# Masking the last 64 queries of each head with GpSimd and an accumulating DMA instead of VectorE

## The chip, the core and the metric

The kernel runs on one core of a Trainium2 chip. The core has a matrix engine (TensorE, PE, with its weight loads shown apart as PEld), a vector engine (VectorE, DVE), a scalar engine for activations (ScalarE, ACT), GpSimd (POOL) and SyncE (SP), which here only starts DMAs. Each engine works through its own queue in order; engines wait for each other by semaphores. Data lie in SBUF (128 partitions) and, for matrix results, in PSUM. The metric is the time of one execution on the device in microseconds (us), as the median of several runs.

## What is computed

Attention over 4 batches of 8 heads, 576 positions, head width 64, with scores far below a row's maximum masked away, then two feed-forward layers:

```python
scores = scale * np.matmul(q, k.transpose(0, 1, 3, 2))
thresh = np.max(scores, axis=-1, keepdims=True) - tau
scores = np.where(scores >= thresh, scores, -1000000000.0)
scores = scores - np.max(scores, axis=-1, keepdims=True)
attn = np.exp(scores)
attn = attn / (np.sum(attn, axis=-1, keepdims=True) + 1e-09)
return np.matmul(attn, v).astype(np.float32)
...
h = x @ w_in
g = np.maximum(h, 0.0) + alpha * np.minimum(h, 0.0)   # second layer: h * sigmoid(h)
return (g @ w_out).astype(np.float32)
```

The feed-forward layers take 2304 tokens of width 512 through 2048 inner columns. Everything is float32.

## The kernel before

The program has two parts that follow each other in each queue: attention, and the two feed-forward layers.

*Units of attention.* Heads are taken two at a time; there are 16 such pairs (`pairs`, index `i`). A unit is a tile of 128 queries or of 2 x 64 queries against all 576 keys. A pair has units `t` = 0 to 7 for its first 512 queries. The last 64 queries of two neighbouring pairs share two more units, `t` = 8 and 9, which are counted with the even `i`; so there are 144 units, and 16 of them have `t` above 7. One unit passes through these steps:

- `qkmm`: PE writes the scores of two units to PSUM (line 576).
- `maxi` (L589, DVE): reads the scores from PSUM, writes them negated and scaled to an SBUF tile `x`, and gathers each row's minimum, which is the maximum of the scores. Four tiles `x` are used in turn (`XB`).
- `thr` (L602, POOL): adds `tau`, for two units at once.
- `expo` (L599, ACT): exponential of `x` into a part of a tile `e`; a tile holds two units, six tiles are used in turn (`EB`).
- `mask` (L608, DVE): sets to zero what lies beyond the threshold, and sums the row.
- `recip` (L614, DVE) and `spread`, `spread8` (L618, L622, POOL copies to `rb`): one over the sum, spread to 64 columns.
- `trans` (L651, PE): transposes of `e` and `rb`, by banks `T0`, `T2`, `T4`, `T6`, `Te` for a pair and `T8`, `T9` for the shared units; `copy` (L307, ACT) brings them to SBUF as `pt`, `pe`, `p8`, `p9`.
- `pv` (L672) and `pv8` (L680), PE: the product with the values; `evac` (L692, L711, ACT) writes it to `X`, and `norm`, `norm8` (L703, L715, POOL) multiply by the reciprocal.

Between them lie parts of the feed-forward layers: the conversion of seven weight tiles (`conv`; on DVE L390, L392 and L394, on POOL L408 and L413), the preparation of the first inputs (`piece`, L445 and L455), and the first four feed-forward products (`h`, line 465). At the very start the PE works on zeros (`idle`, L518): `WU` such fillers ahead of the first scores, `WF` after them.

*What sets the order.* `op(name, engine, duration, priority, dependencies, function, finish)` only records a step. `TABLE1` is a list of numbers that gives the order in which the steps are issued; `plan` walks through it with the durations noted in `op` and so gives each engine its sequence. `ORDER` names the sequence of banks. Steps marked `DVE+` and `POOL+` are those that the planner keeps from running at the same time; in the program that becomes a wait of the POOL step for the `DVE+` step planned before it. A step marked `POOL` gets no such wait. `recip` and `max` are plain `DVE`. The feed-forward layers have `TABLE2` and `SIDE`, which the change leaves as they are.

*The feed-forward layers.* Each runs in groups of inner columns over three parts of 768 tokens, with a scheme of seven products in place of eight; every product is made of three matrix products of split float32 numbers. PE loads weights (L465) for each. Some sums there are made by an accumulating DMA from POOL's queue (L1021).

Of the kernel before, what the change touches and what calls it, by code (L numbers as in the profile page):

```python
# [90 lines left out]
def mode(n):  # L91
# [11 lines left out]
    "352u2x2+BL399+303336FIBMBOBN3A3CFPBPBRHgHf380MBQ0N3FHeBS9-3DHhBUFQBTBVHiHjBX3H3K3BA03NBZBYFR3EBWFS3L"
    "3I3P3G3SHk0IFU3MFJ3JHlFKBaHm3V3a3Q3OHnFV3XBb3T3bBd3R3d3UHo3W3YHpHqFW3fBeBc3iBg013Z3cBh3j3lBi3eFLFX3g"
    "3n3o3k3h3qFYFZBfFTBjHrFaHsHtA1A23tHuBkBmFc3mHv3r3v3yBl3sBn0L3pHwBoBp3z3-44413w3uHxBq3xHy0P42453+Hz0Q"
    "BrFg40Bs47FhH+Fi49Bt4CA34A4F4D0O46434KBuH-48BvBwI0FjBxBy4L4H4N4E4BBzB-B+FbC04SI1I3Fk0TC1I2I4A4I54GC2"
# [1138 lines left out]
```

## Time and profile before

| | us |
|---|---|
| median of 3 runs | 959.94 (959.6 to 960.05) |
| the profiled execution | 959.58 |
| its span in the trace | 957.8 |
| PE busy in the span (modelled ends) | 946.3 |
| PE weight loads busy | 849.6 |
| DVE busy | 843.9 |
| ACT busy | 617.8 |
| POOL busy | 335.1 |

The span runs from the first to the last instruction of one execution; some 1.8 us of the execution lie outside it. Busy shares are averages over both parts of the program: attention lies in the first quarter of the span, up to about 249 us, the feed-forward layers behind it. The granted clock of TensorE is 1.00 of full speed (2.4 GHz) throughout.

### The profile page before, as it was taken

How to read it: one execution, taken by the hardware profiler on the slowest of the kernel's cores; microseconds unless marked ns; L12 is line 12 of the kernel's file. 1: busy time of each engine (PE TensorE's matmuls, PEld its weight loads, DVE VectorE, ACT ScalarE, POOL GpSimd, SP SyncE). 2: the span in 40 equal slices, each digit the busy share in tenths (PEclk: the TensorE clock that was granted, in tenths of full speed). 3: DMA queues.
4: the chain of work that ended last, by engine and by line, in shares of the span. 5: the costliest groups of instructions: out<-in, count | busy, mean ns of one | idle time of the engine just before them, and what ended most of it. 6: DMA issues, size and time to landing. Idle time of an engine off the chain costs nothing.

```text
span 957.8 us, 18332 instructions
## 1 busy us (share of the span) xinstructions
PE 946.3 (99%) x6810; PEld 849.6 (89%) x6810; DVE 843.9 (88%) x1672; ACT 617.8 (65%) x1096; POOL 335.1 (35%) x401
## 2 busy tenths in 40 slices
PE   8999999999999999999999999999999999999998
PEld 4565566665899999999999999999999999999998
DVE  7999999999688668999999999999888888887866
ACT  5889999898767655555555555767664555455442
POOL 0235533445523214453333453301214332323344
PEclk9999999999999999999999999999999999999999
DMA  3132232222667676858667886558685667557543
GB/s 102 35 118 96 77 108 72 70 79 95 227 253 266 241 276 224 274 194 320 230 228 274 261 258 212 184 211 313 241 334 188 242 242 290 177 212 287 178 146 140
DMA packets 46073, 190.99 MB, mean 199 GB/s; under 512 B 5408, under 2 KB 8736, under 8 KB 45984
## 3 DMA queue, kind: packets, MB, share of 16 engines
q1 hardware_dynamic: 44016, 184.81, 54.0%
q0 software_dynamic: 1728, 4.72, 2.7%
q8 instruction: 54, 0.88, 0.4%
q10 hardware_dynamic: 240, 0.30, 0.1%
q14 instruction: 35, 0.29, 0.1%
HBM read 147.33 MB, written 37.75 MB: 193 GB/s over the span
## 4 chain that ended last, share of the span: by engine, by line
PE 93%; DVE 3%; ACT 2%; issue 1%; POOL 0%; DVEq 0%; ACTq 0%; POOLq 0%
PE ab L465 30%; PE c L465 18%; PE y L465 17%; PE s L576 8%; PE pv L672 8%; PE y L958 5%; PE t L651 5%; ACT e L599 1%; PE t L680 1%; PE pv L518 1%; ACT pt L307 1%; DVE x L589 1%; DVE X L975 0%; DVE r L445 0%; DVE e L608 0%
## 5 line engine op out<-in xcount | busy, mean ns | idle before, releaser
L465 PE MATMUL ab<-xs,w 128*128 128x384 f32 x1728 | 326.2, 335 | 0.0
L465 PEld LDWEIGHTS ab<-xs,w 128*128 128x128 f32 x1728 | 302.0, 188 | 2.0 <-DVE e L608 0.8
L465 PE MATMUL y<-g,w 128*128 128x384 f32 x840 | 163.7, 335 | 0.0
L465 PEld LDWEIGHTS y<-g,w 128*128 128x128 f32 x840 | 147.4, 188 | 0.0
L307 ACT ACTIVATE g<-r 128x768 fp32r<-128x768 f32 (+1 forms) x143 | 111.6, 794 | 46.7 <-DVE r L1024 11.5
L408 POOL TENSOR_TENSOR cw<-cw 128x128 f32<-128x128 f32 (+1 forms) x89 | 49.4, 555 | 228.5 <-DVE cw L408 87.8
L307 ACT ACTIVATE su<-ab 128x384 f32<-128x384 f32 x144 | 68.7, 488 | 85.5 <-PE ab L465 66.2
L465 PE MATMUL c<-g,w 128*128 128x384 f32 x612 | 119.8, 335 | 0.0
L608 DVE SCALAR_TENSOR_TENSOR e<-x,m,e 128x577 f32<-128x577 f32 x144 | 116.6, 845 | 0.3 <-POOL m L602 0.2
L589 DVE TENSOR_SCALAR_CACHE_REDUCE x<-s,nsc 128x576 f32<-128x576 f32 x144 | 112.0, 812 | 4.0 <-PE s L576 3.0
L599 ACT ACTIVATE e<-x,m 128x576 f32<-128x576 f32 x144 | 107.9, 779 | 11.5 <-DVE x L589 11.4
L465 PEld LDWEIGHTS c<-g,w 128*128 128x128 f32 x612 | 107.4, 188 | 0.0
L1010 POOL TENSOR_TENSOR g<-r,g 128x768 fp32r<-128x768 f32 x40 | 73.8, 1849 | 74.5 <-DVE cw L408 11.6
L576 PE MATMUL s<-raw 64*128 64x288 f32 (+1 forms) x640 | 98.5, 422 | 0.5 <-DVE x L589 0.4
L975 DVE TENSOR_TENSOR X<-y,X 128x384 f32<-128x384 f32 x150 | 81.2, 551 | 18.7 <-PE y L465 17.9
L651 PEld LDWEIGHTS t<-ident,e 64*128 64x128 f32 x1296 | 56.5, 138 | 46.0 <-ACT pt L307 25.1
L1010 DVE TENSOR_TENSOR g<-r,g 128x768 fp32r<-128x768 f32 x81 | 81.7, 1012 | 4.9 <-ACT g L307 4.8
L465 PE MATMUL c<-xs,w 128*128 128x384 f32 x432 | 84.1, 335 | 0.7 <-ACT r L929 0.7
L576 PEld LDWEIGHTS s<-raw 64*128 64x128 f32 (+1 forms) x640 | 58.6, 177 | 24.8 <-DVE x L589 15.7
L307 ACT ACTIVATE pt<-t 128x512 f32<-128x512 f32 x128 | 71.8, 598 | 9.5 <-PE t L651 9.2
L465 PEld LDWEIGHTS c<-xs,w 128*128 128x128 f32 x432 | 75.7, 188 | 1.1 <-ACT r L929 1.1
L307 ACT ACTIVATE w<-cw 128x896 fp32r<-128x896 f32 (+1 forms) x64 | 59.7, 932 | 24.4 <-POOL cw L408 12.4
(93 smaller groups left out, 1411.3 us busy)
## 6 DMA issues: line engine op xcount, KB each, us to landing
xs<-xd SPq DMA_DIRECT2D x126, 768.0 KB, 5.7
xd<-xs SPq DMA_DIRECT2D x42, 768.0 KB, 4.3
raw<-in_w1i SPq DMA_DIRECT2D x16, 512.0 KB, 5.4
raw<-in_w1o SPq DMA_DIRECT2D x16, 512.0 KB, 5.3
raw<-in_w2i SPq DMA_DIRECT2D x16, 512.0 KB, 5.5
raw<-in_w2o SPq DMA_DIRECT2D x16, 512.0 KB, 4.9
rv<-in_v SPq DMA_DIRECT2D x16, 320.0 KB, 3.3
r<-r POOLq DMA_DIRECT2D x12, 384.0 KB, 5.7
```

The lines of the kernel that those rows point to most:

```text
L307: e.activation(out=dst, in_=src, func=AF.Copy)
L408: st.append((both_step if both else port_step)(256 if len(o.shape) == 3 else 128, ["cv", "ce", "ch"], ["ce"], lambda e=V, o=o, a=a, b=b, o ...
L465: T.matmul(bank, WT_[ws[c]][:, x, AI[a], :], xs[:, y, c, :], start=start and k == 0, stop=stop and k == 5, skip_group_check=True,)
L576: T.matmul(SP[u + k][o, hf, :S // 2], RAW[i + n][p, 0, q], RAW[i + n][p, 1, c], start=True, stop=True)
L589: V.tensor_scalar(out=x.rearrange("p (a b) -> p a b", a=2), in0=SP[u][:, :, :S // 2], scalar1=nsc, scalar2=None, op0=ALU.mult, op1=ALU.min ...
L599: A.activation(out=ES[u], in_=xts[u % XB][:, 1:S + 1], func=AF.Exp, bias=mcol(u, 0), scale=-1.0)
L608: return V.scalar_tensor_tensor(out=e, in0=x, scalar=mcol(u, 1), in1=e, op0=ALU.is_le, op1=ALU.mult, accum_out=mcol(u, 2))
L651: T.transpose(TP[n][h][:, c * 64:c * 64 + 64], x[p], ident[p, p])
L672: T.matmul(AV[i][h * 64:(h + 1) * 64], RV[i][:, h, kt], probs(i, h, kt).rearrange("p a b -> p (a b)"), start=kt == 0, stop=kt == KT - 1)
L958: T.matmul(yt, wview(ws[f])[:, a, i * 128:(i + 1) * 128], half(gs[f, k])[:, c], start=n == 0, stop=n == 3 * G - 1)
L975: V.tensor_tensor(out=dst, in0=src, in1=dst, op=ALU.add))))
L1010: add(*both_step(2 * HN, kr + kg, kg, lambda e: e.tensor_tensor(out=x[:, 1], in0=RP[n], in1=x[:, 0].bitcast(F32), op=ALU.subtract)))
```

## The change

The two shared units of a pair (`t` above 7) no longer use the mask on DVE. In its place, ahead of the exponential: POOL compares the negated scores with the threshold and writes 1e30 where a score is beyond it, zero elsewhere, to a tile `bm` (`above`); a DMA issued by POOL adds `bm` onto the score tile (`raise_`); the exponential of what was raised is zero; and ACT writes the row's sum along with the exponential. POOL then adds 1e-9 to that sum (`eps`), and DVE takes these two reciprocals apart from the other eight (`recip8`). The units have score tiles of their own, two in turn (`PMB`, `xm0` and `xm1`), one single `bm`, and their own tile `e`; the other tiles `e` become five. `sm` has three buffers in place of four. There is one start filler fewer (`WU`). Some durations noted for the planner are other numbers, and `TABLE1` and `ORDER` are new, so the order of the attention part is another on every engine. The order of the feed-forward part is the same.

```diff
 XB = 4
-EB = 6
+EB = 5
+PMB = 2
-WU = 9
+WU = 8
...
-    "P8:1 P8:0 T4:1 Q2:2 P4:0 T6:1 Q4:2 T2:1 Te:1 Q6:2 P0:1 P1:1 Q8:2 T0:2 P2:1 T4:2 Q0:3 P3:1 T2:2 Q2:3 T6:2 P4:1 "
+    "Q2:2 T6:1 P4:0 Te:1 Q4:2 P0:1 P1:1 Q6:2 T8:0 P2:1 T2:2 Q8:2 P3:1 T0:2 Q0:3 T4:2 P4:1 T9:0 Q2:3 P8:0 P8:1 Te:2 "
...
-        sm = ent(name="sm", bufs=4)
+        sm = ent(name="sm", bufs=3)
-        eb = qp.tile([128, EB, 2 * S + 2], F32, tag="e", name="e")
+        eb = qp.tile([128, EB + 1, 2 * S + 2], F32, tag="e", name="e")
...
+        PMU = {u: n for n, u in enumerate(x for x in range(NU) if seq[x][1] > 7)}
+        xms = [rbp.tile([128, S], F32, tag=f"xm{k}", name=f"xm{k}") for k in range(PMB)]
+        bm = rbp.tile([128, S], F32, tag="bm", name="bm")
...
+        def above(u):
+            P.tensor_scalar(out=bm, in0=xt(u), scalar1=mcol(u, 1), scalar2=1e30, op0=ALU.is_gt, op1=ALU.mult)
+
+        def raise_(u):
+            P.dma_start(out=xt(u), in_=bm, accum_op=ALU.add)
+
+        def eps(u):
+            P.tensor_scalar(out=mcol(u, 2), in0=mcol(u, 2), scalar1=1e-9, scalar2=None, op0=ALU.add)
...
-            A.activation(out=ES[u], in_=xts[u % XB][:, 1:S + 1], func=AF.Exp, bias=mcol(u, 0), scale=-1.0)
+            A.activation(out=ES[u], in_=xt(u), func=AF.Exp, bias=mcol(u, 0), scale=-1.0, **({"accum_out": mcol(u, 2)} if u in PMU else {}))
...
         def recip(i):
-            n = 8 if i % 2 else 10
-            V.reciprocal(stat(i)[:, 2, :n], stat(i)[:, 2, :n])
+            V.reciprocal(stat(i)[:, 2, :8], stat(i)[:, 2, :8])
+
+        def recip8(i):
+            V.reciprocal(stat(i)[:, 2, 8:], stat(i)[:, 2, 8:])
...
+            if u in PMU:
+                last = PML[PMU[u] - 1] if PMU[u] else -1
+                op(("above", u), "POOL", 1.93, 2, [("thr", i, t - t % 2), ("raise", last)], lambda u=u: above(u), 2.08)
+                op(("raise", u), "SWD", 0.9, 2, [("above", u)], lambda u=u: raise_(u), 6.5)
+                op(("eps", u), "POOL", 0.2, 2, [("exp", u)], lambda u=u: eps(u), 0.35)
-            op(("exp", u), "ACT", 0.667, 2, [("max", u)] + (users(*etiles[n]) if n >= 0 else []), lambda u=u: expo(u), 0.82)
-            op(("mask", u), "DVE+", 0.74, 2, [("exp", u), ("thr", i, t - t % 2)], lambda u=u: mask(u), 0.9)
+            op(("exp", u), "ACT", 0.667 + 0.19 * (u in PMU), 2, [("max", u)] + [("raise", u)] * (u in PMU) + ring, lambda u=u: expo(u), 0.82 + 0.19 * (u in PMU))
+            if u not in PMU:
+                op(("mask", u), "DVE+", 0.74, 2, [("exp", u), ("thr", i, t - t % 2)], lambda u=u: mask(u), 0.9)
...
-            op(("spread", i), "POOL", 0.6, 1, [("recip", i)] + ([("t", bank[i - 1, "e"])] if i else []), lambda i=i: spread(i), 0.75)
+            op(("spread", i), "POOL", 0.88, 1, [("recip", i)] + ([("t", bank[i - 1, "e"])] if i else []), lambda i=i: spread(i), 1.03)
             if i % 2 == 0:
-                op(("spread8", i), "POOL", 0.25, 1, [("recip", i)] + ([("t", bank[i - 2, "9"])] if i else []), lambda i=i: spread8(i), 0.4)
+                op(("recip8", i), "DVE", 0.12, 0, [("eps", pos[i, x]) for x in (8, 9)], lambda i=i: recip8(i), 0.25)
+                op(("spread8", i), "POOL", 0.46, 1, [("recip8", i)] + ([("t", bank[i - 2, "9"])] if i else []), lambda i=i: spread8(i), 0.6)
```

In the rows below the first number of a name's ending is a buffer: `m_530` before and `m_507` after hold the statistics of pair `i` = 2. First DVE, from the maxima of that pair's shared units on; before:

```order
L589 TENSOR_SCALAR x3_172,m_530<-s_681,nsc_68 128x576
L589 TENSOR_SCALAR x2_169,m_530<-s_680,nsc_68 128x576
L608 SCALAR_TENSOR_TENSOR e_162,m_530<-x0_163,m_530,e_162 128x577
L608 SCALAR_TENSOR_TENSOR e_162,m_530<-x1_166,m_530,e_162 128x577
L589 TENSOR_SCALAR x0_163,m_757<-s_744,nsc_68 128x576
L589 TENSOR_SCALAR x1_166,m_757<-s_745,nsc_68 128x576
L608 SCALAR_TENSOR_TENSOR e_162,m_530<-x3_172,m_530,e_162 128x577
L608 SCALAR_TENSOR_TENSOR e_162,m_530<-x2_169,m_530,e_162 128x577
L589 TENSOR_SCALAR x3_172,m_757<-s_781,nsc_68 128x576
L589 TENSOR_SCALAR x2_169,m_757<-s_780,nsc_68 128x576
L614 RECIPROCAL m_530<-m_530 128x10
```

The same place on DVE after the change:

```order
L609 TENSOR_SCALAR xm1_187,m_507<-s_674,nsc_68 128x576
L609 TENSOR_SCALAR xm0_186,m_507<-s_673,nsc_68 128x576
L636 RECIPROCAL m_211<-m_211 128x2
L628 SCALAR_TENSOR_TENSOR e_162,m_507<-x3_172,m_507,e_162 128x577
L609 TENSOR_SCALAR x1_166,m_745<-s_715,nsc_68 128x576
L609 TENSOR_SCALAR x0_163,m_745<-s_714,nsc_68 128x576
L628 SCALAR_TENSOR_TENSOR e_162,m_507<-x2_169,m_507,e_162 128x577
L633 RECIPROCAL m_507<-m_507 128x8
L609 TENSOR_SCALAR x2_169,m_745<-s_759,nsc_68 128x576
L609 TENSOR_SCALAR x3_172,m_745<-s_760,nsc_68 128x576
```

The two masks of the shared units are gone; the reciprocal of the pair before's shared units stands between the maxima and a mask.

POOL at that place, before (thresholds L602, copies of reciprocals L618 and L622, products with the reciprocal L703 and L715):

```order
L602 TENSOR_SCALAR m_530<-m_530,ptau_67 128x2 x2
L602 TENSOR_SCALAR m_757<-m_757,ptau_67 128x2
L618 COPY rb_836<-m_530 128x512
L703 TENSOR_TENSOR X0_69<-X0_69,pe_663 128x256
L602 TENSOR_SCALAR m_757<-m_757,ptau_67 128x2 x2
L622 COPY rb8_892<-m_530 128x128
```

And after (comparison L538, its DMA L541; thresholds L622, copies L640 and L644, products L725 and L737):

```order
L622 TENSOR_SCALAR m_507<-m_507,ptau_67 128x2 x2
L644 COPY rb8_721<-m_211 128x128
L538 TENSOR_SCALAR bm_188<-xm0_186,m_507 128x576
L541 DMA xm0_186<-bm_188 128x576
L640 COPY rb_771<-m_507 128x512
L622 TENSOR_SCALAR m_745<-m_745,ptau_67 128x2 x2
L737 TENSOR_TENSOR X0_69<-X0_69,p9_766 128x2x64
L725 TENSOR_TENSOR X0_69<-X0_69,pe_602 128x256
L622 TENSOR_SCALAR m_745<-m_745,ptau_67 128x2
L538 TENSOR_SCALAR bm_188<-xm1_187,m_507 128x576
L541 DMA xm1_187<-bm_188 128x576
```

Two comparisons and two DMAs have come in, ahead of copies and thresholds of the pairs that follow.

ACT, from the exponential of unit `xm0` of that pair on, after the change (before, the two stand as `e_162<-x3_172,m_530` and `e_162<-x2_169,m_530`, four rows apart and ahead of all exponentials of the next pair):

```order
L619 ACTIVATE e_162,m_507<-xm0_186,m_507 128x576
L390 ACTIVATE cw_84<-raw0_83 128x512
L308 ACTIVATE pt_890<-t_946 128x8x64
L619 ACTIVATE e_162<-x0_163,m_936 128x576
L308 ACTIVATE pt_890<-t_947 128x8x64
L308 ACTIVATE pt_890<-t_975 128x8x64
L619 ACTIVATE e_162<-x1_166,m_936 128x576
L308 ACTIVATE pt_890<-t_976 128x8x64
L714 ACTIVATE X0_69<-pv_887 128x512
L619 ACTIVATE e_162,m_507<-xm1_187,m_507 128x576
```

The two exponentials now stand behind all eight of the next pair (`m_745`), and the second behind two of the pair after that (`m_936`).

PE at the end of attention, before, up to the feed-forward layers:

```order
L680 MATMUL t<-p_3501,rv 64x64 x8
L680 MATMUL t<-p_3587,rv 64x64 x2
L672 MATMUL pv<-pt,rv 64x512 x2
L465 MATMUL ab_3647<-xs_79,w_72 128x384 x3
L465 MATMUL ab_3647<-xs_79,w_73 128x384 x3
L651 MATMUL t<-ident,e 128x64 x16
L672 MATMUL pv<-pe,rv 64x512 x2
```

and after:

```order
L673 MATMUL t<-ident,rb 128x64 x8
L694 MATMUL pv<-pt,rv 64x512 x8
L673 MATMUL t<-ident,e 128x64 x16
L694 MATMUL pv<-pe,rv 64x512 x2
L673 MATMUL t<-ident,e 128x64 x2
L673 MATMUL t<-ident,rb_3774 128x64 x2
L466 MATMUL ab_3650<-xs_80,w_74 128x384 x3
L466 MATMUL ab_3650<-xs_80,w_75 128x384 x3
L702 MATMUL t<-p_3780,rv 64x64 x8
L702 MATMUL t<-p_3798,rv 64x64 x2
```

The products of the last shared units (L680, now L702) stood ahead of the last pair's last banks, and now stand with their transposes at the very end; of the four early feed-forward products one has moved forward.

## Rows read from the trace of the kernel before

**Rows 1.** Windows: us, busy us (instructions) of each engine, granted clock, DMA.

```profile
core 0: us, PE busy (x) PEld busy (x) DVE busy (x) ACT busy (x) POOL busy (x), PEclk, DMA share, GB/s
40.00:60.00 20.00, 19.37 (x200) 10.55 (x199) 19.90 (x54) 17.69 (x31) 5.75 (x13) 1.00 0.26 78
120.00:140.00 20.00, 19.96 (x254) 12.92 (x252) 20.00 (x53) 18.26 (x35) 7.67 (x18) 1.00 0.27 77
200.00:220.00 20.00, 19.93 (x260) 12.16 (x258) 19.94 (x54) 19.30 (x38) 10.73 (x24) 1.00 0.21 65
260.00:280.00 20.00, 20.00 (x117) 20.00 (x116) 18.11 (x31) 16.20 (x34) 3.97 (x4) 1.00 0.61 246
```

**Rows 2.** Waits of DVE, 20 to 235 us: for whom, us, times, longest.

```profile
DVE x L589 <- PE s L576: 0.7, 2, 0.6
DVE x L589 <- PE t L651: 0.2, 1, 0.2
DVE e L608 <- POOL m L602: 0.2, 1, 0.2
```

**Rows 3.** Chain of waits, 22 to 245 us, shares by line.

```profile
by line: PE pv L672 30.8%; PE s L576 30.5%; PE t L651 22.2%; PE t L680 3.5%; ACT e L599 3.2%; ACT pt L307 2.8%; issue 2.0%; PE ab L465 1.1%; DVE x L589 0.8%; POOL cw L408 0.5%; ACT pe L307 0.5%; ACT w L307 0.4%; DVE e L608 0.4%; DVE cw L394
```

**Rows 4.** Groups by line and shape, 10 to 240 us: count, busy, mean ns, idle before.

```profile
L608 DVE SCALAR_TENSOR_TENSOR e<-x,m,e 128x577 f32<-128x577 f32 x143 | 115.9, 845 | 0.3 <-POOL m L602 0.2
...
L703 POOL TENSOR_TENSOR X<-X,pe 128x256 f32<-128x256 f32 x12 | 8.7, 735 | 9.4 <-DVE e L608 9.4
...
L703 POOL TENSOR_TENSOR X<-X,pe 128x192 f32<-128x192 f32 x12 | 7.2, 596 | 7.6 <-DVE e L608 7.6
```

**Rows 5.** Lines L608 (masks) and L618 (copies): shortest, median, longest ns.

```profile
L608 DVE SCALAR_TENSOR_TENSOR e<-x,m,e x144: 757/816/1271, 10.5 to 240.0; 128x577 f32<-128x577 f32 x144
...
L618 POOL COPY rb<-m x16: 609/988/1196, 24.7 to 241.2; 128x512 f32<-128x512 f32 x16
```

**Rows 6.** Timeline of attention, DVE and POOL: start us, us, what.

```profile
142.96 0.61 POOL L618 COPY rb<-m 128x512 f32<-128x512 f32 x1
...
143.78 0.29 POOL L622 COPY rb<-m 128x128 f32<-128x128 f32 x1
...
163.15 0.81 DVE L608 SCALAR_TENSOR_TENSOR e<-x,m,e 128x577 f32<-128x577 f32 x1
...
163.89 0.81 DVE L608 SCALAR_TENSOR_TENSOR e<-x,m,e 128x577 f32<-128x577 f32 x1
...
172.75 0.21 DVE L614 RECIPROCAL m<-m 128x10 f32<-128x10 f32 x1
...
173.01 0.82 DVE L608 SCALAR_TENSOR_TENSOR e<-x,m,e 128x577 f32<-128x577 f32 x1
173.12 1.17 POOL L618 COPY rb<-m 128x512 f32<-128x512 f32 x1 [0.69 <-DVE m L614]
...
173.75 1.16 DVE L608 SCALAR_TENSOR_TENSOR e<-x,m,e 128x577 f32<-128x577 f32 x1
```

**Rows 7.** Timeline of the feed-forward stage, DVE and POOL.

```profile
361.91 1.84 POOL L1010 TENSOR_TENSOR xs<-r,xs 128x768 fp32r<-128x768 f32 x1 [1.14 <-DVE r L1024]
...
362.69 1.88 DVE L1010 TENSOR_TENSOR g<-r,g 128x768 fp32r<-128x768 f32 x1
```

**Rows 8.** Line L1021, the accumulating DMAs of POOL's queue.

```profile
L1021 POOL DMA_DIRECT2D r<-r x12: 862/874/1399, 370.4 to 599.5; - x12
...
DMA to landing us min/median/max: 3.9/5.7/10.6
```

**Rows 9.** Timeline of the start, PE's first instructions.

```profile
1.18 4.02 PE L518 MATMUL pv<-cw 128*128 128x512 bf16 x9 [1.18 <-DVE cw L492]
...
5.13 0.96 PEld L576 LDWEIGHTS s<-raw 64*128 64x128 f32 x8 [0.84 <-DMA raw<-in_k]
```

**Rows 10.** Timeline of the end of attention, PE.

```profile
236.70 1.39 PE L680 MATMUL t<-p,rv 128*64 128x64 f32 x40
...
238.88 1.34 PE L465 MATMUL ab<-xs,w 128*128 128x384 f32 x6
...
241.80 0.72 PE L651 MATMUL t<-ident,e 64*128 64x64 f32 x16
```

More of the change, by code (lines that the diff above doesn't have):

```diff
@@ L103 @@
[L103 to L106, printed above, removed]
-    "4TFdC34PFpC4I64MA54I4JFe4VI7C54QC60S4a4X4OC7C8I84R4UI9IA4d4f4iC9CBFl4W4YFqIB4b4l4Z4cFrFfCA4eCCCE4n4q"
@@ L124 @@
+    "JRJSJqJy9nJrFUFWJsJtJT9s9rFVJzJu9m01I4B3I7B4I8I9IAJUFXJVI5IBJwFYFaFZICFbIEIDJWK2FcJ+I6HxHyHz"
 )
@@ L492, in attn_moe_moe @@
         V.memset(zero, 0.0)
-        eb = qp.tile([128, EB, 2 * S + 2], F32, tag="e", name="e")
-        ets = [eb[:, i] for i in range(EB)]
+        eb = qp.tile([128, EB + 1, 2 * S + 2], F32, tag="e", name="e")
+        ets = [eb[:, i] for i in range(EB + 1)]
         xts = []
@@ L524, in op, with xtile_, xt @@
             ops[name] = (eng, dur, dur + 0.2 if fin is None else fin, deps, fn)
+        PMU = {u: n for n, u in enumerate(x for x in range(NU) if seq[x][1] > 7)}
+        xms = [rbp.tile([128, S], F32, tag=f"xm{k}", name=f"xm{k}") for k in range(PMB)]
+        bm = rbp.tile([128, S], F32, tag="bm", name="bm")
+        def xtile_(u):
+            return xts[(u - sum(x < u for x in PMU)) % XB]
+        def xt(u):
+            return xms[PMU[u] % PMB] if u in PMU else xtile_(u)[:, 1:S + 1]
+        def above(u):
[4 more added lines that the diff above has]
+            P.tensor_scalar(out=mcol(u, 2), in0=mcol(u, 2), scalar1=1e-9, scalar2=None, op0=ALU.add)
         KS, RV, RAW, HI, SP, ES, EP, MS, TP, PT, AV, RS = ({} for _ in range(12))
@@ L587, in maxi @@
         def maxi(u):
-            x = xts[u % XB][:, 1:S + 1]
+            x = xt(u)
             V.tensor_scalar(
@@ L746, in attn_moe_moe, with past, masked @@
             load(i)
-        etiles = [(i, t // 2) for i, t in seq if t % 2 == 0]
+        etiles = [(i, t // 2) for i, t in seq if t % 2 == 0 and t < 8]
         eidx = {x: n for n, x in enumerate(etiles)}
+        PML = sorted(PMU)
+        def past(u):
+            if u in PMU:
+                return [("exp", PML[PMU[u] - PMB])] if PMU[u] >= PMB else []
+            n = [x for x in range(NU) if x not in PMU]
+            k = n.index(u) - XB
+            return [("mask", n[k]), ("exp", n[k])] if k >= 0 else []
+        def masked(u):
+            return ("exp" if u in PMU else "mask", u)
         for u in range(NU):
@@ L753, in attn_moe_moe @@
                 op(("thr", i, t), "POOL+", 0.3, 0.5, [("max", u), ("max", u + 1)], lambda i=i, t=t: thr(i, t), 0.4)
-            op(("max", u), "DVE", 0.74, -1, [qk(u), ("tauv",), ("mask", u - XB), ("exp", u - XB), ("spread", i - 4), ("spread8", i - 4)], lambda u=u: maxi(u), 0.86)
-            n = eidx[i, t // 2] - EB
-            op(("exp", u), "ACT", 0.667, 2, [("max", u)] + (users(*etiles[n]) if n >= 0 else []), lambda u=u: expo(u), 0.82)
-            op(("mask", u), "DVE+", 0.74, 2, [("exp", u), ("thr", i, t - t % 2)], lambda u=u: mask(u), 0.9)
+            op(("max", u), "DVE", 0.74, -1, [qk(u), ("tauv",), *past(u), ("spread", i - 3), ("spread8", i - 3)], lambda u=u: maxi(u), 0.86)
@@ L758, in attn_moe_moe @@
+            op(("exp", u), "ACT", 0.667 + 0.19 * (u in PMU), 2, [("max", u)] + [("raise", u)] * (u in PMU) + ring, lambda u=u: expo(u), 0.82 + 0.19 * (u in PMU))
+            if u not in PMU:
+                op(("mask", u), "DVE+", 0.74, 2, [("exp", u), ("thr", i, t - t % 2)], lambda u=u: mask(u), 0.9)
         for i in range(NP):
-            op(("recip", i), "DVE", 0.12, 0, [("mask", pos[i, x]) for x in range(8 if i % 2 else 10)], lambda i=i: recip(i), 0.25)
-            op(("spread", i), "POOL", 0.6, 1, [("recip", i)] + ([("t", bank[i - 1, "e"])] if i else []), lambda i=i: spread(i), 0.75)
+            op(("recip", i), "DVE", 0.12, 0, [("mask", pos[i, x]) for x in range(8)], lambda i=i: recip(i), 0.25)
@@ L763, in attn_moe_moe @@
         for n, (i, kind) in enumerate(banks):
             need = {
-                "e": [("mask", pos[i, x]) for x in range(8)] + [("spread", i)],
-                "9": [("mask", pos[i, x]) for x in (8, 9) if (i, x) in pos] + [("spread8", i)],
-            }.get(kind) or [("mask", pos[i, int(kind) + x]) for x in range(2)]
+                "e": [masked(pos[i, x]) for x in range(8)] + [("spread", i)],
+                "9": [masked(pos[i, x]) for x in (8, 9) if (i, x) in pos] + [("spread8", i)],
+            }.get(kind) or [masked(pos[i, int(kind) + x]) for x in range(2)]
```

58 lines of the change are left out of this document (32 added, 26 removed), and 24 rows, old and new, of the table ORDER.

## Prediction, written before the changed kernel was run

> **What bounds the kernel now.** I read the stages first [rows 1]. In three stretches of 20 us between 40 and 220 us, all of them attention, VectorE (DVE) is busy 19.9 to 20.0 us, TensorE (PE) 19.4 to 20.0 by its modelled ends, ScalarE (ACT) 17.7 to 19.3, and GpSimd (POOL) 5.8 to 10.7. From 260 us on, in the two feed-forward layers, the PE has no gap and loads weights without a break (20.00 of 20), while DVE has room (18.1). So a shorter attention stage brings everything behind it forward by the same amount, since the order of the later work is not changed, and nothing done to DVE later would help. Then I ask who sets the pace inside attention. DVE's own waits there come to 1.1 us in 215 [rows 2]: it is limited by its work. The chain of waits over 22 to 245 us is 88.1% PE (30.8 + 30.5 + 22.2 + 3.5 + 1.1) [rows 3], so of these 223 us some 26 are steps in which the PE waited for another engine. Two engines share the bound: DVE, which is full, and the PE, which can give back 26 us at the very most. Whatever DVE saves can only arrive through those 26 us.
>
> **What is removed.** Sixteen of 144 masks leave DVE: the two with queries 512 to 575 in each of eight pairs of heads. Masks that follow each other start 0.74 us apart (163.15 to 163.89) [rows 6], so 16 x 0.74 = 11.8 us.
>
> **What DVE gets in exchange.** The reciprocal of ten columns becomes one of eight and, for each pair, one of two. The reciprocal at 172.75 holds the next mask back to 173.01 [rows 6], 0.26 us. Eight more are 2.1 us. DVE's own work falls by 9.7 us.
>
> **What POOL gets, and how that comes back to DVE.** POOL gets 16 comparisons over 576 columns (`above`), 16 DMA issues and 16 small additions. POOL itself has room [rows 1]; the price lies in what a POOL instruction does to a mask that it meets. A mask reads two SBUF tensors. At 173.12 POOL's copy of 512 columns began under one mask and took 1.17 us, where 0.61 is its time alone, and the mask that started at 173.75 took 1.16 instead of 0.81 [rows 6]. In the feed-forward stage the block is complete: POOL runs from 361.91 to 363.75, a DVE instruction with two tensors starts at 362.69 and takes 1.88 [rows 7], so it ended 0.82 after POOL let go. The kernel avoids this for most POOL work by a wait on a chosen mask; the copies have no such wait, and `above` has none either. So I price `above` by the copies. All masks together are stretched by (845 - 816) ns x 144 = 4.2 us, mean against median [rows 4, 5]. The copies' own work is 16 x 0.61 + 8 x 0.29 = 12.1 us [rows 5, 6]. That makes 0.35 us of stretch for each us of unguarded POOL work, if the copies caused it all.
>
> How long `above` takes no row shows. Like the copy it reads one tensor and writes one: 0.61 x 576 / 512 = 0.69 us as the lower end. The upper end is POOL's two-input form: 596 ns at 192 columns and 735 at 256 [rows 4], 2.17 ns a column, 1.43 us at 576. The change's own planner books 1.93. I take the middle of the two rows, 1.06, since it is one tensor with two operations. Stretch: 16 x 1.06 x 0.35 = 5.9 us, with 3.9 and 8.0 at the ends, and 10.8 at 1.93.
>
> The Trainium skill (GPSIMD Engine Reference, section 3.1) says that a POOL body of up to two operations runs at about 1.03 cycles an element at 1.2 GHz, by which I estimate 0.49 us for 576 columns and a fixed part; that points to the lower end, and with 3.9 us of stretch the sum below would be 954.4 instead of 956.4. The same page's section 1 speaks against the change: SBUF is shared between the two engines where a DVE instruction has two SBUF inputs; the mask stretched to 1.16 us agrees.
>
> **What ACT gets.** Sixteen exponentials also write their sum. DVE's reads of an accumulator overlap at 0.08 us; the change books 0.19. That is 1.3 to 3.0 us in all. ACT has 0.7 to 2.3 us idle in each 20 [rows 1], some 14 us over nine such stretches, so I take zero; with that cover gone it is 3.0.
>
> **The new chain for the last 64 queries.** Maximum, threshold, `above`, a DMA that adds the result onto the scores, exponential. A POOL-issued accumulating DMA holds POOL for 0.87 us and lands 5.7 us after its issue at the median, 3.9 to 10.6 [rows 8], with 384 KB where this one has 288. The two of a pair come one after the other, since the buffer `bm` is single: 0.5 + 1.06 + 0.3 + 5.7 = 7.6 us to the first, 14.7 to the second. In ACT's new order the first of these exponentials stands about 16 DVE instructions (12 us) after its maximum, the second about 20 (15 us). So the first has 4 us in hand and the second next to nothing. On the PE the transposes of these tiles stand 26 or more steps behind their scores, over 22 us. I take zero. Queued behind a late landing would be ACT's copies after the exponential, and on POOL, behind the small addition that waits for it, the thresholds of the next tiles, for which DVE's masks wait.
>
> The Trainium skill (DMA: Bandwidth & Descriptors, the section on the anatomy of a SWDGE transfer) fits such a transfer at 2.0 us plus bytes / 436e3, an estimate of 2.7 us here; the shortest landing in this trace, 3.9 us, does not reach it, and by that rule no landing would be late.
>
> **Fillers and the tail.** One start filler fewer is worth up to 0.4 us, but the first scores already waited for the landing of `in_k` at 5.13 [rows 9]; I take zero. At the end the last pair's transposes and products move behind the last mask (0.72 for sixteen transposes, a quarter of that for four, 1.39 for the products), and one early feed-forward product (1.34) moves ahead of it [rows 10]: +1.0 us at most, none if the PE has the time anyway; +0.6 taken.
>
> **The sum.** The profiled run took 959.58 us, of which the span is 957.8. Minus 9.7, plus 5.9, plus 0.6 is -3.2: 956.4 in that run, and as the median of the three runs lies 0.36 higher, 956.7.
>
> **Rivals.** *The block decides (slower).* The place is the mask behind each `above`. A threshold takes 0.29 us and starts some 0.2 after a mask, so `above` starts about 0.5 after it; two maxima, which read PSUM, cover 1.48 us. At 1.93 us `above` ends at 2.43 and holds the next mask for 0.95: 16 x 0.95 = 15.2, so -9.7 + 15.2 + 0.6 = +6.1, 966.0. It decides from 9.7 / 16 = 0.61 us a piece. For it: the complete block in rows 7, and that `above` waits for no mask. Against: the copies cost 4.2 / 24 = 0.18 each. *No stretch at all.* At 0.69 us `above` fits into the shadow of two maxima (0.5 + 0.69 < 1.48) and the fillers' 0.4 is gained: -10.1, 949.8. Against it: the copies, shorter still, do stretch masks. *Nothing passes through.* DVE gets free time, but the PE (88% of the chain) and ACT (up to 19.3 of 20) keep the stage: 959.9. *Late landings (slower).* The second exponential has no slack; each us that all eight come late costs up to 8 us on ACT: -3.2 + 8, 964.7.
>
> **How the numbers follow.** By how far the rows bear each out: forecast 0.38, no stretch 0.13, nothing passes 0.20, block 0.19, late landings 0.10. About 0.2%, 1.9 us, is what a measurement of this kernel can tell from no change. The forecast's own range is 954 to 959, so a little of it falls inside that: faster 0.50, same 0.22, slower 0.28. The range for 8 in 10 goes from 950, close to the no-stretch case, to 966, the block.
>
> **What would show it.** In the trace of the changed kernel: `above` between 0.7 and 1.4 us (longer counts for the block); the masks' mean against their median times 128, some 10 us in sum, where 4.2 stands now; idle time on DVE appearing in the windows of the attention stage, ended by PE or ACT; waits of the exponentials for a DMA, which should be absent; and the first feed-forward products without gaps some 3 us earlier. I am wrong if DVE stays at 19.9 of 20 with as long a stage, if ACT or POOL waits for landings, or if the PE's tail after the last mask grows by more than 1 us.

## The result, and the profile after

The changed kernel takes 966.75 us (median of six runs, 965.11 to 967.11) beside 959.9 for the one before on the same chip: a ratio of 1.0068, 95% interval 1.0055 to 1.0081. It is slower by 0.7%, where I had predicted 956.7 and faster, and lies just outside my range of 950 to 966. The profiled execution took 966.19 us with a span of 964.4, which is 6.6 us more than before.

First the same windows as in [rows 1] (us, busy us and instructions of each engine, clock, DMA).

```profile
40.00:60.00 20.00, 19.20 (x255) 12.24 (x257) 18.88 (x51) 17.30 (x34) 10.69 (x18) 1.00 0.35 98
120.00:140.00 20.00, 20.00 (x220) 12.05 (x217) 19.71 (x53) 18.83 (x36) 14.12 (x23) 1.00 0.29 83
200.00:220.00 20.00, 19.91 (x232) 12.13 (x230) 18.71 (x50) 18.11 (x35) 14.70 (x22) 1.00 0.53 134
260.00:280.00 20.00, 20.00 (x117) 20.00 (x116) 19.41 (x34) 15.79 (x33) 4.67 (x3) 1.00 0.67 272
```

VectorE (third pair) has fallen from 19.9 to 20.0 down to 18.7 to 19.7: it has gaps now. GpSimd (fifth) has risen by 4.0 to 6.5 us in the three stretches of attention. In the feed-forward stage TensorE is as full as before. What ends VectorE's gaps, as in [rows 2] (for whom, us, times, longest):

```profile
DVE e L628 <- POOL m L622: 4.7, 7, 1.3
DVE x L609 <- PE s L596: 2.8, 7, 0.6
DVE xm L609 <- PE s L596: 2.4, 4, 1.4
DVE e L628 <- ACT e L619: 1.3, 2, 1.1
DVE x L609 <- PE t L673: 0.5, 1, 0.5
```

That is 11.7 us where 1.1 stood. The largest is new: masks (L628) wait for a threshold (`thr`, L622), GpSimd's addition over two columns. The chain of waits of [rows 3] now reads:

```profile
by line: PE s L596 16.5%; PE pv L694 14.4%; PE t L673 10.8%; issue 10.3%; DVE e L628 8.4%; POOL bm L538 7.5%; DMA xm<-bm 6.5%; DVE x L609 5.8%; POOL m L622 3.2%; POOL X L725 2.9%; POOL w L414 2.0%; ACT e L619 1.8%; ACT pt L308 1.7%; POOL xm
```

The scores, products and transposes of TensorE had 83.5% of the attention chain and have 41.7%. The comparison `above` (L538, `bm`), the landing of its DMA and the thresholds have 17.2% between them. The new instructions by line (shortest, median, longest ns; then the landing in us), and the masks as in [rows 5]:

```profile
L538 POOL TENSOR_SCALAR bm<-xm,m x16: 2217/2221/2703, 21.5 to 240.9; 128x576 f32<-128x576 f32 x16
...
L541 POOL DMA_DIRECT2D xm<-bm x16: 892/922/1067, 24.0 to 243.6; - x16
...
DMA to landing us min/median/max: 3.4/4.3/7.3
...
L628 DVE SCALAR_TENSOR_TENSOR e<-x,m,e x128: 800/816/1322, 11.0 to 244.3; 128x577 f32<-128x577 f32 x128
```

`above` takes 2.22 us, twice the 1.06 I took and over my upper row of 1.43. With the issue (0.92), each of the 16 shared units takes some 3.2 us of GpSimd. One place shows what that does (timeline; start us, us, what):

```profile
165.47 2.58 POOL L538 TENSOR_SCALAR bm<-xm,m 128x576 f32<-128x576 f32 x1
...
165.89 1.29 DVE L628 SCALAR_TENSOR_TENSOR e<-x,m,e 128x577 f32<-128x577 f32 x1
...
167.11 0.81 DVE L628 SCALAR_TENSOR_TENSOR e<-x,m,e 128x577 f32<-128x577 f32 x1
...
168.11 0.29 POOL L644 COPY rb<-m 128x128 f32<-128x128 f32 x1
168.35 0.94 POOL L541 DMA_DIRECT2D xm<-bm  x1
...
168.78 0.82 DVE L609 TENSOR_SCALAR_CACHE_REDUCE x<-s,nsc 128x576 f32<-128x576 f32 x1
169.01 1.59 POOL L414 TENSOR_TENSOR w<-cw,w 128x224 fp32r<-128x224 f32 x2
...
170.28 0.60 POOL L622 TENSOR_SCALAR m<-m,ptau 128x2 f32<-128x2 f32 x1
170.52 0.90 POOL L640 COPY rb<-m 128x512 f32<-128x512 f32 x1
170.91 1.14 DVE L628 SCALAR_TENSOR_TENSOR e<-x,m,e 128x577 f32<-128x577 f32 x1 [1.31 <-POOL m L622]
```

The last maximum ends at 169.60. Its threshold stands on GpSimd behind the comparison, a copy, the DMA issue and two pieces of a weight block, and starts at 170.28. VectorE idles 1.31 us. Of the two masks that run inside the comparison only the one at 165.89, early in it, is stretched; the one at 167.11 takes its usual 0.81.

### The profile page after: what moved, and what is told of

The parts are those of the page before. It is cut to its first block, busy times and chain, and to the rows that moved or that the text cites. A ratio compares the mean times of both kernels' runs of the same rounds, so it can differ in the third digit from the quotient of the medians.

```text
span 964.4 us, 18338 instructions
## 1 busy us (share of the span) xinstructions
PE 951.8 (99%) x6809; PEld 850.8 (88%) x6809; DVE 837.8 (87%) x1648; ACT 620.4 (64%) x1112; POOL 395.5 (41%) x449
## 4 chain that ended last, share of the span: by engine, by line
PE 81%; DVE 7%; POOL 5%; issue 3%; DMA 3%; ACT 1%; POOLq 0%; DVEq 0%; ACTq 0%
PE ab L466 29%; PE c L466 18%; PE y L466 17%; PE y L999 5%; PE s L596 5%; PE pv L694 4%; PE t L673 3%; DVE e L628 2%; POOL bm L538 2%; DMA xm<-bm 2%; DVE x L609 1%; DMA r<-r 1%; POOL m L622 1%; PE pv L519 1%; POOL X L725 1%
## 5 line engine op out<-in xcount | busy, mean ns | idle before, releaser
L628 DVE SCALAR_TENSOR_TENSOR e<-x,m,e 128x577 f32<-128x577 f32 x128 | 106.5, 861 | 7.0 <-POOL m L622 5.2
L619 ACT ACTIVATE e<-x,m 128x576 f32<-128x576 f32 x128 | 96.7, 782 | 13.6 <-DVE x L609 12.0
L609 DVE TENSOR_SCALAR_CACHE_REDUCE x<-s,nsc 128x576 f32<-128x576 f32 x128 | 99.4, 809 | 6.8 <-PE s L596 5.5
L596 PE MATMUL s<-raw 64*128 64x288 f32 (+1 forms) x640 | 102.4, 426 | 1.5 <-DVE x L609 1.5
L1016 DVE TENSOR_TENSOR X<-y,X 128x384 f32<-128x384 f32 x150 | 81.2, 550 | 18.7 <-PE y L466 17.9
```

What stands on the lines that cost most here:

```text
L596: T.matmul(SP[u + k][o, hf, :S // 2], RAW[i + n][p, 0, q], RAW[i + n][p, 1, c], start=True, stop=True)
L609: V.tensor_scalar(out=x.rearrange("p (a b) -> p a b", a=2), in0=SP[u][:, :, :S // 2], scalar1=nsc, scalar2=None, op0=ALU.mult, op1=ALU.min ...
L619: A.activation(out=ES[u], in_=xt(u), func=AF.Exp, bias=mcol(u, 0), scale=-1.0, **({"accum_out": mcol(u, 2)} if u in PMU else {}))
L628: return V.scalar_tensor_tensor(out=e, in0=x, scalar=mcol(u, 1), in1=e, op0=ALU.is_le, op1=ALU.mult, accum_out=mcol(u, 2))
L1016: V.tensor_tensor(out=dst, in0=src, in1=dst, op=ALU.add))))
```

## The experiments

Theories: **Q**, GpSimd's held queue makes thresholds late; **P**, the comparison holds masks at the SBUF port (my rival "the block decides"); **O**, the new order and tables are worse by themselves; **L**, exponentials wait for the landing. Ratios are to the kernel before on the same chip, with 95% intervals.

**The comparison on 64 columns.**

```
-  P.tensor_scalar(out=bm, in0=xt(u), ...)
+  P.tensor_scalar(out=bm[:, :64], in0=xt(u)[:, :64], ...)
```

> The changed kernel with the comparison of each shared unit cut from 576 columns to 64 on GpSimd (the rest of the 1e30 mask stays zero, so most of the last 64 queries' keys are left unmasked); order, DMA and waits are unchanged. The changed kernel has 966.75 us, the one before 959.9. GpSimd's comparison takes 2.22 to 2.70 us there and should fall to about 0.4. Theory Q (GpSimd's queue: 16 comparisons of 2.3 us make the thresholds late and VectorE waits for them): about 31 us leave GpSimd and the time falls to 961 or under. Theory P (the comparison holds VectorE's masks at the shared port): only the 1.6 us by which the masks stretch more than before come back, 965. Theory O (the new order of work is worse by itself): 966 to 967. Theory L (exponential waits for the landing of the accumulating DMA, above all in the last pair): each landing comes 1.9 us earlier, so 963 to 965.

Measured 958.21, ratio 0.9978 (0.9968 to 0.9987): 8.5 us back. O falls, and so does L as the only cause. The masks of the two kernels (count, busy us and mean ns, idle before), changed and then narrow:

```profile
L628 DVE SCALAR_TENSOR_TENSOR e<-x,m,e 128x577 f32<-128x577 f32 x128 | 106.5, 861 | 7.0 <-POOL m L622 5.2 <-ACT e L619 1.3
```

```profile
L629 DVE SCALAR_TENSOR_TENSOR e<-x,m,e 128x577 f32<-128x577 f32 x128 | 102.0, 827 | 2.4 <-POOL m L623 1.6 <-POOL m L545 0.6
```

128 x 34 ns = 4.4 us less stretch, and 3.6 us less waiting for thresholds (5.2 to 1.6): P and Q both remain.

**A held queue without the wide comparison.** Narrow, then eight or six additions of one column.

```
+  for k in range(8):   # 6 in the second run
+      P.tensor_scalar(out=junk, in0=mcol(u, 1), scalar1=1.0, op0=ALU.add)
```

> The narrow comparison (64 columns; 958.2 us) followed each time by eight additions of one column on GpSimd, 8 x 0.22 = 1.8 us, so that its queue is held about as long as by the full comparison (2.33 us; 966.75), while almost nothing is read or written that VectorE could meet at the port (the last 64 queries are mostly not masked). Theory Q (the held queue makes thresholds late): 965 to 967. Theory P (the wide read and write hold VectorE's masks): 958 to 960. Half and half, as the traces put it (4.3 us of mask stretch, 3.6 us of waits for thresholds): 961 to 963.

> The narrow comparison followed by six additions of one column on GpSimd instead of eight: 0.68 + 6 x 0.283 = 2.38 us of GpSimd per shared unit, as long as the full comparison's 2.33, with next to nothing read or written at the port (the last 64 queries are mostly not masked). Theory Q (held queue): 966 to 969, the full comparison's 966.75 or a little over. Theory P (port): 958 to 960. Both in halves: 961 to 963.

Measured 977.28 (ratio 1.0182, 1.0165 to 1.0199) with eight and 969.93 (1.0102, 1.0085 to 1.0119) with six. Both lie above Q's own ranges, 965 to 967 and 966 to 969. One reason is in the traces: the additions don't follow each other at once. With six, a unit's comparison and additions are busy 0.63 + 6 x 0.305 = 2.46 us, but from the start of the first to the end of the last pass 2.95, as 0.08 us lie idle ahead of each addition. That is 0.6 more than the full comparison's 2.33, and the time is 3.2 us over the changed kernel's. With eight it is 2.93 busy and 3.59 in all. VectorE's first wait with six, the additions by line, and the same as a group (busy, mean ns, idle before):

```profile
DVE e L632 <- POOL m L626: 9.8, 13, 2.0
```

```profile
L542 POOL TENSOR_SCALAR junk<-m x96: 207/209/1290, 21.1 to 246.7; 128x1 f32<-128x1 f32 x96
```

```profile
L542 POOL TENSOR_SCALAR junk<-m 128x1 f32<-128x1 f32 x96 | 29.3, 305 | 7.9
```

Twice the wait for thresholds. So holding the queue makes a loss of this size without the wide comparison; Q stands. How much of the 8.5 us it makes at exactly 2.33 us I can only estimate: 8.5 on a straight line between the narrow run and the one with six additions, 6.4 on a parabola through these two and the one with eight. It isn't free of the port either: an addition of one column takes 209 ns at the median and up to 1290 beside a mask, and the masks still average 848 (827 in the narrow run).

**A wait before the comparison.** Here `above` waits for the last mask issued, as the thresholds do.

```
-  elif c == "POOL+" and held is not seen:
+  elif (c == "POOL+" or c == "POOL" and x is not None and held is not None) and held is not seen:
```

> The changed kernel, computing the same, with each comparison on GpSimd made to wait for the mask that was issued last on VectorE, as the thresholds and the normalisations do; nothing else moves. In the changed kernel the masks take 861 ns each and with the narrow comparison 827, that is 128 x 0.034 = 4.3 us. Theory P: no mask meets a comparison's first half microsecond any more, or fewer do, and up to 4 us come back: 962 to 965. Theory Q: GpSimd's comparison starts up to 0.8 us later and its queue gets later still: 967 to 970.

Measured 969.25 (1.009, 1.0073 to 1.0107). The masks' mean fell only from 861 to 855 ns, and the waits for thresholds rose from 5.2 to 9.3 us:

```profile
L628 DVE SCALAR_TENSOR_TENSOR e<-x,m,e 128x577 f32<-128x577 f32 x128 | 105.7, 855 | 11.0 <-POOL m L622 9.3 <-ACT e L619 1.3
```

The guard left most of the stretch in place, so it doesn't price P by itself. But over the seven runs in the table of the next section the time follows the waits for thresholds and not the masks' mean: 862 ns and 962.76 us with the DMA to unused memory, 847 ns and 977.28 with eight additions. P falls as the main cause; what part of its 4.4 us passes to the time is not shown.

**The landing.** The DMA writes to unused memory; alone, and with the narrow comparison.

```
-  P.dma_start(out=xt(u), in_=bm, accum_op=ALU.add)
+  P.dma_start(out=bmx[:, PMU[u]], in_=bm)
```

> The changed kernel with the DMA of each shared unit writing the 1e30 mask to unused memory instead of adding it to the scores, so the exponentials of the last 64 queries don't wait for a landing (and are not masked); comparison, GpSimd issue and order stay. Theory L: the 6.5 us that the chain of waits puts on the landing and about 2 us of the tail come back: 959 to 962. Theory Q: GpSimd's queue is as full as before: 965 to 967. Theory P: 966 to 967. Theory O: 966 to 967.

> Both cuts at once on the changed kernel: the comparison on 64 columns and the DMA to unused memory, so neither GpSimd's 2.3 us nor the landing holds anything (the last 64 queries are not masked); the order, the tables, the DMA issue on GpSimd and the eight extra reciprocals stay. The single cuts measured 958.2 and 962.8 against 966.75, 8.5 and 4.0 us. If comparison and landing are costs in series (each link of mask, DMA, exponential counted): 954 to 955. If they cover each other and the rest of the time is that of the order and of the other engines (theory O and PE as the next bound): 957 to 959.

Measured 962.76 (1.0027, 1.0017 to 1.0037) and 957.59 (0.9979, 0.997 to 0.9988). The first lies between the ranges of L and Q. So the landing costs up to 4.0 us behind a full comparison and 0.6 behind a narrow one; it is dear only where the comparison makes it late. The 4.0 aren't all waits of exponentials: the write to memory also holds GpSimd 0.29 us less at its issue (0.64 for 0.93, means), and the small addition no longer stands behind a late exponential; the waits for thresholds fell with it:

```profile
DVE e L629 <- POOL m L623: 2.4, 6, 1.0
```

**No DMA at all**, with the narrow comparison.

```
-  P.dma_start(out=xt(u), in_=bm, accum_op=ALU.add)
+  return None
```

> The narrow comparison and no DMA at all (the last 64 queries are not masked): against the comparison with the DMA to unused memory (957.6) only the 16 issues on GpSimd, 0.64 to 0.93 us each, leave. If the issue holds the thresholds as the comparison does (8.5 us for 16 x 1.65 us of GpSimd): 16 x 0.64 = 10 us of GpSimd, so 3 us, 954 to 955. If TensorE bounds what is left (955.9 with VectorE's masks nearly gone as well): 956 to 957.6.

Measured 957.7 (0.9975, 0.9966 to 0.9984). Against the narrow comparison with the DMA to unused memory (957.59) the issue costs nothing that shows. This is about what the change could be worth if GpSimd's part cost next to nothing: 2.5 us.

**VectorE relieved.** Masks of 64 columns, in the changed kernel (with the narrow comparison) and in the one before.

```
+  e, x = (e[:, -64:], x[:, -64:]) if o else (e[:, :64], x[:, :64])
```

> The changed kernel with the narrow comparison and with VectorE's 128 masks cut from 577 columns to 64 (most keys are left unmasked): VectorE loses 128 x 0.7 = 85 us of work, so it can't be the bound of the attention stage any more. Narrow alone measured 958.2. If VectorE bounds the stage over all its length, as the idle time of 0.1 us between its instructions suggests: the stage shrinks by tens of us, below 930. If TensorE and ScalarE, which stand at 18.5 to 20 of 20 us in every stretch, are right behind it: 950 to 957, and the 10 us of VectorE work that the change takes out could never have passed to the time.

> The kernel before, in its own order, with its 144 masks cut from 577 columns to 64 (most keys are left unmasked): VectorE loses 144 x 0.56 = some 80 us of work and nothing else changes. If VectorE bounded the stage, as the prediction read it from its 18.5 to 19.9 busy us in 20, tens of us go: under 930. If TensorE bounds it, as the chain of waits of the kernel before says (88% on TensorE's lines) and as the changed kernel with the same cut did (955.9): 956 to 959, and no saving on VectorE could have brought more than 1 to 4 us.

Measured 955.93 (0.9958, 0.9943 to 0.9973) and 954.99 (0.9943, 0.9929 to 0.9957). The kernel before without 80 us of VectorE work, in a window and in the chain of waits:

```profile
200.00:220.00 20.00, 20.00 (x248) 12.40 (x246) 12.81 (x55) 18.94 (x36) 9.00 (x20) 1.00 0.16 48
```

```profile
by line: PE pv L673 32.9%; PE s L576 30.2%; PE t L652 21.9%; PE t L681 4.1%; ACT pt L307 3.5%; ACT e L599 2.6%; PE ab L465 1.6%; issue 1.1%; DVE x L589 0.8%; ACT X L693 0.5%; ACT w L307 0.4%; ACT cw L389 0.3%; ACT pe L307 0.2%; ACT X L712 0
```

VectorE is busy 12.8 of 20 and the stage gains 5 us; the chain is nearly the one of [rows 3]. In the kernel before, TensorE set the pace all along.

**The comparison elsewhere or cheaper.** On VectorE; with one operation; behind the next threshold; and the last two together.

```
-  P.tensor_scalar(out=bm, ..., scalar2=1e30, op0=ALU.is_gt, op1=ALU.mult)
+  V.tensor_scalar(...)                       # first run
+  ..., scalar2=None, op0=ALU.is_gt)          # second
+  pend.append(u)  # comparison and DMA issued after the next thr: third, fourth
+  P.dma_start(out=xt(x), in_=bm.bitcast(I32), accum_op=ALU.add)   # fourth
```

> The changed kernel with the comparison of each shared unit on VectorE (tensor_scalar from one SBUF tile to another) instead of GpSimd; the accumulating DMA stays with GpSimd. No row shows this instruction on VectorE: between 0.3 us and the mask's 0.82 us, so 16 x 0.3 to 0.8 = 5 to 13 us more of VectorE, and 16 x 2.3 = 37 us less of GpSimd. Theory Q: the waits for thresholds (some 8 to 10 us) and the tail's comparison leave: 959 to 964. Theory O: 971 to 979. Theory P: 969 to 975. Theory L: 966 to 972.

> The changed kernel with GpSimd's comparison in one operation (greater than, without the product with 1e30, so the sums are raised by 1 and the last 64 queries not masked); all else stays. If GpSimd's time goes with the number of operations in the instruction: about 1.3 us for 576 columns instead of 2.33, and some 60% of the 8.5 us that the 64 columns gave back: 961 to 962.5. If it goes with the columns alone: 2.3 us and 966 to 967.

> The changed kernel, computing the same, with each comparison and its DMA put behind the next threshold on GpSimd instead of right behind its own; nothing else moves. Theory Q: a threshold is needed every 3.3 us and comparison and issue take 2.33 + 0.93 = 3.3, so a comparison that starts right behind a threshold is out of the next one's way: 962 to 965. Theory P: the masks meet the comparisons as before: 966 to 967; and up to 3 us later landings could cost 1 to 3 us, 968.

> As the one with the comparison behind the next threshold, computing the same, but the comparison has one operation (greater than), and its 1.0 is handed to the accumulating DMA as the integer of the same bits, which raises the scores by 1.07e9. The single operation alone measured 962.35 (1.88 us on GpSimd instead of 2.33). Theory Q: 959 to 962. Theory P: 962 to 963. If the conversion in the DMA slows the landing beyond 3.4 to 7.3 us: 964 to 968.

Measured: on VectorE 963.19 (1.0032, 1.0022 to 1.0043); one operation 962.35 (1.0023, 1.0014 to 1.0032); deferred 990.28 (1.0321, 1.0304 to 1.0339); deferred with one operation 979.54 (1.0204, 1.0189 to 1.0219). The run on VectorE lies in Q's range alone, though VectorE has 16 x 0.53 = 8.5 us more work in it. The one with one operation lies in the first range, but the comparison fell to 1.74 and not to 1.3. On VectorE and with one operation on GpSimd it takes

```profile
L538 DVE TENSOR_SCALAR bm<-xm,m x16: 508/518/701, 21.1 to 238.6; 128x576 f32<-128x576 f32 x16
```

```profile
L538 POOL TENSOR_SCALAR bm<-xm,m x16: 1722/1736/2317, 22.9 to 239.0; 128x576 f32<-128x576 f32 x16
```

All expectations for the deferred runs missed, Q's too: the highest was 968 for each, 22 and 12 us too low. In the deferred run the masks still wait 4.2 us for thresholds (4.7 in the changed kernel), and what else is queued behind the comparison comes late too: TensorE's transposes wait for the copy of the reciprocals (`rb`), and exponentials for the landing.

```profile
PE t L681 <- POOL rb L648: 13.5, 7, 3.4
```

```profile
ACT e L627 <- DMA xm<-bm: 6.2, 6, 2.8
```

Part of the miss is TensorE's clock. In five places of the deferred run the granted clock fell from 2.4 to 1.2 GHz, for 20.5 us in all, each time behind a gap of 1.8 to 3.4 us in TensorE's work (another gap of 2.4 us had no fall behind it). One window of it:

```profile
180.00:200.00 20.00, 16.20 (x204) 11.02 (x202) 12.87 (x35) 13.07 (x27) 11.74 (x14) 0.83 0.23 57
```

At half the clock at most half of such a stretch is lost, so up to some 10 of the 22 us by which the ranges were too low (an estimate). With one operation it is 6.8 us at 1.2 GHz.

GpSimd's queue has several customers; moving the comparison out of one's way put it into another's. No version here is faster than the kernel before and computes the same.

**The comparison in the old order.**

```
+  if t == 8 or t == 0 and i % 2:   # behind the threshold
+      P.tensor_scalar(out=bm, in0=cz, ...)
```

> The kernel before in its own order, with 16 comparisons of 576 columns added on GpSimd (on a constant tile, the result unused), one behind the threshold of every query tile 8 and one behind that of the first tile of every second pair. Nothing waits for them but GpSimd's queue, and VectorE where the two share the SBUF port. Before is 959.9. If what the narrow cut gave back (8.5 us) is the price of the comparison itself wherever it stands (theories Q and P together): 966 to 969. If it costs only VectorE's stretch at the port, 16 x 0.3 = 4 to 5 us, with VectorE as the bound: 963 to 965. If only the new order is sensitive to it: 960 to 961.

Measured 978.19 (1.0182, 1.0157 to 1.0208), more than any theory said. Transposes wait for the copies `rb`, some of which stand right behind:

```profile
PE t L659 <- POOL rb L626: 7.3, 4, 2.9
```

Here too the clock has a part: the four runs go from 974.11 at a mean granted clock of 0.998 to 980.13 at 0.991. Even the fastest is 14 us over the kernel before. An order that doesn't plan for the comparison suffers more from it, so it isn't the new order that makes it dear.

**VectorE masks in the new order**, tried twice: at the place of GpSimd's small addition, and at the place of the comparison, with the exponential ahead of them.

```
+  V.scalar_tensor_tensor(out=ES[u], in0=xt(u), scalar=mcol(u, 1), in1=ES[u], op0=ALU.is_le, op1=ALU.mult, accum_out=mcol(u, 2))
```

> The changed kernel's order, tables and tiles, but the last 64 queries are masked by 16 VectorE instructions after their exponentials as in the kernel before (comparison and DMA left out, GpSimd's small add too). VectorE gets 16 x 0.82 = 13 us back, and the 10 to 11 us of new idle time, the 1.6 us of extra stretch and some 2 us of the tail have no cause left if they came from GpSimd or the DMA. Theories Q and L: the order is sound, and the time is that of the kernel before plus eight reciprocals and what an order planned for other work costs: 960 to 964. Theory O: the order is the cause and carries the new masks on top: 970 to 978. Theory P: 962 to 966.

Measured 968.76 (1.0086, 1.0071 to 1.0101). This lies in no theory's range, between P's and O's. These masks came behind the transposes that read the tile (one wait of 0.8 us for them), so this isn't the undoing it was meant to be. What it shows is that the new order with 16 more masks on VectorE is slower than the old one.

> The changed kernel's order, tables and tiles, computing the same, but the last 64 queries' exponential and then their mask on VectorE stand where the changed kernel has the comparison on GpSimd, ahead of the transposes that read them; no comparison, no accumulating DMA. This undoes the new mask and keeps the new order, as the earlier kernel with VectorE masks meant to (in that one the masks stood behind the transposes and waited for them: 968.8, which says little). VectorE has the work of the kernel before and eight short reciprocals. Theory O (the new order is worse by itself): 966 or more. Order sound, loss from GpSimd and the landing: 958 to 963.

Measured 983.25 (1.0232, 1.0217 to 1.0248). VectorE waits 8.9 us in front of these masks for exponentials that had to move with them, and TensorE had 10 us at 1.2 GHz. So I found no way to run the new order with the old masks, and these two runs leave open what it would cost then. The narrow runs at 957.6 to 958.2 show what matters here: with a short comparison on GpSimd the order is sound.

**One filler fewer**, in the kernel before (`WU = 8`).

> The kernel before with one filler product fewer (8 instead of 9) ahead of the first scores, the one part of the change that stands alone. The prediction put it at zero (0 to -0.4 us): 959.5 to 960. If the first scores wait for the fillers: 959.6. If the fillers kept the clock up: 960 to 961.

Measured 960.24 against 960.06 (1.0001, 0.9992 to 1.001): nothing, as predicted.

## Why the prediction was wrong, by its own steps

**"Whatever VectorE saves can only arrive" through TensorE's 26 us, taken as room for all of it: failed.** I saw [rows 3] with 88.1% on TensorE beside a VectorE without gaps [rows 1, 2] and counted the -9.7 in full. With 80 us off VectorE the kernel before gains 5.1 us. So by that run no more could pass, and by the run without a DMA 2.5 did. My rival "nothing passes" (0.20) described the saving better than the forecast. A full engine next to one that holds the chain is not a second bound until the chain passes through it: of VectorE's lines [rows 3] shows 0.8 and 0.4%.

**"POOL itself has room": failed, and this turned the sign.** I priced POOL only by what it does to a mask it meets, and the queue at zero. Only behind a late landing did I let thresholds come late; that the comparison itself holds them up was not in the sum. Most of GpSimd's work in attention is of the kind that others wait for: thresholds for masks, copies for transposes, normalisations. By the runs in the new order: how long the comparison, or what stands for it, holds GpSimd in each unit (mean, from its start to the last end), VectorE's waits for thresholds from 20 to 235 us, the masks' mean, and the time:

| held, us | run | waits, us | masks, ns | time, us |
|---|---|---|---|---|
| 0.68 | 64 columns | 0.8 | 827 | 958.2 |
| 1.88 | one operation | 1.9 | 850 | 962.4 |
| 2.38 | the change, DMA to unused memory | 2.4 | 862 | 962.8 |
| 2.33 | the change | 4.7 | 861 | 966.75 |
| 2.40 | the change, guarded | 6.8 | 855 | 969.25 |
| 2.95 | 64 columns, six additions | 9.8 | 848 | 969.9 |
| 3.59 | 64 columns, eight additions | 16.8 | 847 | 977.3 |

The time rises with the waits for thresholds in every row; the masks' mean doesn't order it. The waits are a sign of the held queue and not its whole price: between the first row and the change they grow by 3.9 us, the time by 8.5. From 0.68 to 1.88 a microsecond of hold in each of the 16 units costs 3.5 us, from 2.95 to 3.59 it costs 11: a queue that fills up. The runs are from several chips; the kernel before took 959.9 to 960.2 on each.

GpSimd was busy 5.8 to 10.7 of 20 in [rows 1], 14.1 and 14.7 in the later two windows after. An average share with room says little of a queue that is served in order.

**The length of `above`: mis-sized.** 1.06 us taken (0.69 to 1.43 by rows), 2.22 measured (2.33 as a mean). The change's planner, at 1.93, was nearer than either row.

**The stretch, +5.9: near in size by luck.** The full comparison stretches the masks by 4.4 us against the narrow one, within 3.9 to 8.0, but two misses cancel: it ran twice as long as taken, and the rate was 4.4 / (16 x 2.33) = 0.12 us per us, not 0.35. As a change against the kernel before it was too high: mean less median comes to 128 x 45 ns = 5.8 us where 4.2 stood and some 10 were forecast.

**The rival "the block decides" gave 966.0, close to the time, for the wrong reason.** Its mechanism, a mask held until `above` ends, isn't in the trace: no mask that meets a comparison takes over 1.32 us, the one at 167.11 ran in 0.81, and the run with a guard was slower. The complete block that I cited for it [rows 7] is under a GpSimd instruction with two inputs; the comparison has one.

**"Late landings" (0.10): partly.** Exponentials wait twice for a landing (1.7 us), and the runs give up to 4.0 us, thresholds and issue included, where I had taken zero; behind a narrow comparison it is 0.6. The landing itself was faster than I took, 4.3 at the median instead of 5.7.

**Fillers at zero** held. **The tail, +0.6:** from the last mask to the first feed-forward product of line `c` it grew from 10.1 to 12.1 us.

```profile
250.96 2.24 PE L465 MATMUL c<-xs,w 128*128 128x384 f32 x12
```

```profile
244.28 0.82 DVE L628 SCALAR_TENSOR_TENSOR e<-x,m,e 128x577 f32<-128x577 f32 x1
```

```profile
257.16 1.15 PE L466 MATMUL c<-xs,w 128*128 128x384 f32 x5 [0.38 <-ACT X L733]
```

The first is before (its last mask starts at 240.0 [rows 5] and ends at 240.84), the others after. This is over the 1 us that I had named as a sign of being wrong. But the distance is 11.9 us in the narrow run too, which is faster, so the tail doesn't explain the loss. **ACT at zero** was not tried apart; its 16 sum reads take 0.20 us each (median).

The sum by runs, across chips: 960.2 (before, beside the run without a DMA), minus 2.5 that pass (957.7), plus 0.5 for issue and landing behind a narrow comparison (958.2), plus 8.5 for the full one: 966.7. The 8.5 hold the late thresholds, the later landings and the stretch together.

## What to carry to other kernels

When two engines look full, look at the chain's shares (here they gave the right answer), and cut the other engine's work on the chip to be sure: one such run (masks of 64 columns) would have capped the gain at 5 us. Before moving work to an engine with a low share, list what else stands in its queue, who waits for each item, and how long the longest new item holds them up. Here moving the long item only changed which of them came late.
